# A state-space scan and a GELU feed-forward in one kernel: the first four chunks loaded, scaled and turned in two halves of 64 partitions

## The chip, the cores and the metric

The kernel runs on one core of one Trainium2 chip. The metric is device time in microseconds of one execution, as the median of several runs. A core has a matrix engine (TensorE, in the profile PE, with its weight loads PEld), a vector engine (VectorE, DVE), a scalar engine (ScalarE, ACT), a general engine (GpSimd, POOL) and a queue that issues most transfers (SyncE, SP). Each engine runs its instructions in order; between engines only semaphores order the work. Matrix results land in PSUM, which has eight banks of 128 partitions x 2 KB; VectorE and ScalarE copy them ("evict" them) to the on-chip memory SBUF.

## What is computed

Two parts follow each other. The first is a scan with 4 batches, 8 heads, 768 positions, head size 32 and state size 16. With `cum` the running sum of `log a` inside a chunk it is

```python
CB = np.einsum('bhin,bhjn->bhij', Cc, Bc)
M = CB * L                       # L = exp(cum_i - cum_j), causal
y_intra = np.einsum('bhij,bhjd->bhid', M, xc)
y_inter = np.einsum('bhin,bhnd->bhid', Cc, state) * decay_to_i[:, :, :, None]
y[:, :, sl] = y_intra + y_inter
state = decay_full[:, :, None, None] * state + np.sum(Bx, axis=2)
...
x = np.ascontiguousarray(attn_out.transpose(0, 2, 1, 3)).reshape(B * S, H * D)
h = x @ w_in                     # 3072 x 256 by 256 x 2048
out = gelu_tanh(h) @ w_out       # 3072 x 2048 by 2048 x 256
```

The second part is most of the arithmetic: two matrix products of 3072 x 256 x 2048 each.

## The kernel before

**Tiling.** The 3072 positions are 24 chunks of 128, six to a batch, and 12 units of two chunks. A unit u passes through these steps, whose names are used from here on:

- G.u: C times B for both chunks and eight heads, into the four banks `ga` and `gb` (line 603); M.u.0 and M.u.1 multiply the two pairs of banks by the causal mask on VectorE (line 613). For unit 0 alone the second pair goes another way: GE copies a bank on ScalarE (line 618) and ME masks the copy on GpSimd (line 624) or VectorE (line 627).
- D.u gives the chunk's addition to the state; S.c updates the state of chunk c, SP.c spreads it by heads (lines 684 and 691, VectorE).
- Y.u adds M times x and C times state in bank `yb` (lines 658, 667); yev.u evicts it as bf16 into `xm`.
- s1.u.i, i = 0 to 7: four matmuls of 256 columns with two of the sixteen 128-column blocks of `w_in` (line 717) into one of two banks `hp`; gelu.u.i empties it (line 721).
- s2.c.q, q = 0 to 3: four matmuls of 256 columns with a quarter of `w_out` (line 735); oev.c evicts, store.c writes to HBM. s2.c.q needs the gelus 2q and 2q+1 of its unit and quarter q of `w_out`.

So there are 384 s1 and 384 s2 matmuls. Quarter q of `w_in` (load_wi.q, casts wi.q.0 and wi.q.1) is needed by s1.u.2q; the same for `w_out` with load_wo.q, wo.q.0 and wo.q.1.

**How B, C and x come in.** Batch 0 is split: chunks 0 to 3 are loaded first (load_bc0.1 for C, load_bc0.0 for B, load_x4 for x), with four neighbouring positions on each of the 128 partitions; chunks 4 and 5 follow (load_bc1). `a` comes twice: as `aq` for the first 512 positions, one chunk on 32 partitions, and as `a_t` for all, half a sequence on 32 partitions. clipq, Rq (a scan), tpq (a transpose) and recip0 make the weights from `aq`; mulc.0, mulc.1 and mulb scale C (in two masked copies) and B; tw.1, tw.2 and tw.0 turn them by TensorE through `ident`, ew evicts; x is cast (x4), and XX.u spreads it by a 0/1 matrix `unp` to the chunks' order, XD.u stands for D.u, xn.c evicts. clip, R, tp6, recip, pe, pp, pend do the same from `a_t` for the rest. Batch 1 is turned on TensorE (mul, T, E, F, N, bn), batches 2 and 3 by transposing transfers (load_wr, load_tr, load_bn).

**What sets the order.** The text ORDERED lists every step once. Each engine gets its steps in that order. `name:E` puts a step on another engine (A ScalarE, D VectorE, P GpSimd); `~n` are n idle blocks of 128 columns of a zero weight on TensorE; `+n` are idle blocks inside an s1 step. Steps that are not named otherwise run on the engine given in `add`. Transfers of `load_*` are issued from SP, or from ScalarE with `:A`.

Up to s1.2.0, the first feed-forward matmuls of unit 2, the order before names two s2 steps (s2.0.0.0 and s2.0.1.0). All of unit 0's s2 steps go by quarters over its two chunks into one bank `o_ps`; from unit 1 on a chunk's four quarters follow each other.

Of the kernel before, what the change touches and what calls it, by code (L numbers as in the profile page):

```python
# [23 lines left out]
load_bc1.0 load_wo.0 wi.3.0:D gelu.0.1 wi.2.1 s1.0.3 load_x.2 SP.2 pe wi.3.1 gelu.0.2 load_bc.1.1  # L24
gelu.0.3 tp6.2 s1.0.4 load_bc.1.0 gelu.0.4 load_x.3 load_wo.1 xn.3 s1.0.5 s1.0.6 Y.1 gelu.0.5 pp
tp2 gelu.0.6 tp6.3 recip1 s1.0.7 S.1.1 yev.1.0.2 mul1.0:P mul1.1:P tp6.1 pend gelu.0.7 s1.1.0
wo.0.1 T1.0 s1.1.1 T1.1 gelu.1.0 bh1 N1 gelu.1.1 s1.1.2 tp6.0 s1.1.3+10 bn1 ce1.1 load_wo.2
castx.2.None SP.3 wo.0.0 ce1.0 gelu.1.2 gelu.1.3 G.2 s1.1.4 recip.1.4 s1.1.5 gelu.1.4 M.2.1
mul.1.1:P s2.0.0.0.o D.2 M.2.0 load_x.4 gelu.1.5 s2.0.1.0.o s1.1.6 T.1.1 gelu.1.6 S.2.0 s1.1.7
SP.4 Y.2 mul.1.0 yev.2.0.2:D gelu.1.7 wo.1.0 wo.1.1 T.1.0 E.1.1:A castx.3.None:A s1.2.0 wo.2.0  # L30
s1.2.1 E.1.0 wo.2.1 load_wo.3 load_bc.2.1 N.1 gelu.2.0 F.1 s1.2.2 bn.1:D G.3 gelu.2.1 gelu.2.2 D.3
s1.2.3 s2.0.0.1.o S.3.0 S.3.1 load_bc.2.0 gelu.2.3 s1.2.4 M.3.1 s2.0.1.1.o s1.2.5 SP.6 gelu.2.4
s1.2.6 M.3.0 gelu.2.5 wo.3.0:D gelu.2.6 s2.0.0.2.o castx.4.None s1.2.7 Y.3 gelu.2.7 wo.3.1:D
s2.0.1.2.o S.4.0 yev.3.0.2 S.4.1 s2.0.0.3.o oev.0 load_x.5 s1.3.0 s1.3.1 mul.2.1 s2.0.1.3.o
load_wr.2.1 load_x.6 gelu.3.0 gelu.3.1 s1.3.2 oev.1:D SP.8 s1.3.3 s2.1.0.0.o gelu.3.2 M.4.0
gelu.3.3 SP.7 s2.1.0.1.o s2.1.0.2.o s2.1.0.3.o oev.2:D s1.3.4 s1.3.5 s2.1.1.0.o gelu.3.4 M.4.1
mul.2.0:P castx.5.None:A s2.1.1.1.o Y.4 S.5.0 s2.1.1.2.o load_wr.2.0 s2.1.1.3.o load_tr.2.1
load_bn.2 oev.3:D gelu.3.5 s1.3.6 s1.3.7 s2.2.0.0.o yev.4.0.2 load_tr.2.0 gelu.3.6 s1.4.0 SP.9
M.5.1 gelu.3.7 s2.2.0.1.o store.0 store.2 gelu.4.0 s1.4.1 castx.6.None:A s1.4.2 SP.10 s2.2.0.2.o
load_x.7 s2.2.0.3.o gelu.4.1 oev.4:D gelu.4.2 s1.4.3 s1.4.4 load_bc.3.1 s2.2.1.0.o s2.2.1.1.o  # L40
s2.2.1.2.o gelu.4.3 gelu.4.4 s2.2.1.3.o s1.4.5 oev.5 s1.4.6 gelu.4.5 M.5.0 s2.3.0.0.o F.2 store.1
Y.5 s2.3.0.1.o s2.3.0.2.o yev.5.0.2 gelu.4.6 s2.3.0.3.o s1.4.7 S.6.0 gelu.4.7 load_bc.3.0 S.6.1
store.3 s1.5.0 oev.6:D SP.12 s2.3.1.0.o gelu.5.0 s1.5.1 s2.3.1.1.o gelu.5.1 castx.7.None:A
mul.3.1:P s2.3.1.2.o s1.5.2 gelu.5.2 M.6.1 s2.3.1.3.o s1.5.3 M.6.0 Y.6 oev.7:D S.7.0 gelu.5.3
load_x.8 s1.5.4 S.7.1 s2.4.0.0.o s2.4.0.1.o s1.5.5 SP.13 gelu.5.4 load_wr.3.1 yev.6.0.2
castx.8.None store.4 load_x.9 gelu.5.5 SP.14 s2.4.0.2.o s2.4.0.3.o oev.8 s1.5.6 s1.5.7 mul.3.0
castx.9.None s2.4.1.0.o gelu.5.6 load_wr.3.0 gelu.5.7 M.7.0 s2.4.1.1.o s1.6.0 M.7.1 load_tr.3.1
# [38 lines left out]
def kernel(  # L86
# [62 lines left out]
    def load_bc0(i):  # L149
        nc.sync.dma_start(out=BC0[0][:, i], in_=(B, C)[i][0, :, 0:R4 * Q, :]  # L150
                          .rearrange("h (p r) n -> p h (r n)", r=R4))
# [5 lines left out]

    def load_aq(i, eng):
        (nc.scalar if eng == "ACT" else nc.sync).dma_start(out=aq_t[32 * i:32 * i + 32], in_=a_rows(i * Q, Q))  # L159
# [22 lines left out]
    def load_x4():  # L182
        nc.sync.dma_start(out=x4_t, in_=x[0, :, 0:R4 * Q, :].rearrange("h (p r) d -> p h (r d)", r=R4))  # L183
# [35 lines left out]
    def c_wz():  # L219
        nc.vector.memset(wz, 0.0)  # L220

    def c_zero():
# [5 lines left out]
        nc.vector.memset(unp, 0.0)
# [755 lines left out]
```

## Time and profile before

| | |
|---|---|
| median of 3 runs | 118.47 us (118.43 to 118.48) |
| span of the profiled execution | 116.9 us |
| TensorE clock granted | 1.00 throughout |
| TensorE matmul / weight load busy | 110.1 us / 92.0 us |
| VectorE / ScalarE / GpSimd busy | 69.4 us / 72.1 us / 21.4 us |
| DMA | 42,800 packets and 15.64 MB on SP's queue |

The profile gives no time of the profiled execution other than its span; what lies around the span is seen only in the difference to the runs.

How to read it: the span runs from the first to the last instruction of the core. In a line of the timeline the first number is the start, the second the length, then come the engine (SPq and ACTq are the transfers that SP and ScalarE issue), the line of the kernel, the operation with its output and inputs, their shapes, how many are merged into the line, and in brackets the idle time ahead of it with what ended it. Matmuls overlap: each has a latency of some 0.2 us beyond its share of the stream, so eight that follow each other closely show a length that is longer than the time they take up. The chain of waits gives that time.

### The profile page before, as it was taken

What the parts mean: (1) busy time and instruction counts of PE and PEld (TensorE: products, weight loads), DVE (VectorE), ACT (ScalarE), POOL (GpSimd) and SP (SyncE); (2) the same over time, 40 slices, a digit from 0 to 9 for tenths busy, and PEclk for the clock granted to TensorE, in tenths of its full rate; (3) what the DMA queues carried; (4) which work ended last, traced back from release to release, by engine and by line L of the source; (5) the groups of instructions that cost most, each with busy time, mean ns of one, the idle gap of its engine ahead of it and who ended that gap; (6) DMA issues with size and microseconds to landing.
All of it is one profiled execution on the core that took longest, in us unless ns stands there. A gap on an engine that the chain in (4) does not pass through costs nothing.

```text
span 116.9 us, 3379 instructions
## 1 busy us (share of the span) xinstructions
PE 110.1 (94%) x1426; PEld 92.0 (79%) x1426; DVE 69.4 (59%) x140; ACT 72.1 (62%) x139; POOL 21.4 (18%) x38
## 2 busy tenths in 40 slices
PE   6988999998899999999999999999999999999990
PEld 2354676776789979989898999889798998999970
DVE  5898899899785936716695583049493462101020
ACT  2249899968486459565766677828465587447501
POOL 7606816908206000052200000000000000000000
PEclk9999999999999999999999999999999999999999
DMA  0999997999983929998407472044201201101113
GB/s 26 228 332 357 281 252 178 208 288 257 305 143 90 185 47 219 213 253 200 72 25 171 121 163 63 0 140 98 40 6 63 71 0 52 43 0 50 45 47 132
DMA packets 43007, 15.97 MB, mean 137 GB/s; under 512 B 36657, under 2 KB 41457, under 8 KB 42993
## 3 DMA queue, kind: packets, MB, share of 16 engines
q1 hardware_dynamic: 42800, 15.64, 56.0%
q8 instruction: 11, 0.18, 0.6%
q10 hardware_dynamic: 192, 0.13, 0.5%
q14 instruction: 4, 0.02, 0.1%
HBM read 11.04 MB, written 3.93 MB: 128 GB/s over the span
## 4 chain that ended last, share of the span: by engine, by line
PE 75%; DMA 8%; DVE 6%; SPq 6%; issue 2%; POOL 1%; ACT 0%; DVEq 0%; POOLq 0%
PE o_ps L735 33%; PE hp L717 30%; DMA bcf<-in_B_dram 8%; PE yb L735 3%; SPq L190 3%; PE ga L603 3%; PE yb L658 2%; DVE m L613 2%; PE yb L667 2%; DVE ce L523 1%; SPq L150 1%; DVE bh L327 1%; DVE bc L484 1%; SPq L159 1%; SPq L183 1%
## 5 line engine op out<-in xcount | busy, mean ns | idle before, releaser
L721 ACT ACTIVATE gT<-hp 128x512 bf16<-128x512 f32 x96 | 54.3, 596 | 25.0 <-PE hp L717 24.6
L717 PE MATMUL hp<-xm,w_in_sb 128*128 128x256 bf16 x384 | 53.3, 273 | 0.6 <-ACT gT L721 0.4
L735 PE MATMUL o_ps<-w_out_sb,gT 128*128 128x256 bf16 x352 | 47.3, 273 | 0.0
L717 PEld LDWEIGHTS <-w_in_sb 128*128 128x128 bf16 x384 | 41.4, 114 | 3.5 <-issue 1.9
L735 PEld LDWEIGHTS <-gT 128*128 128x128 bf16 x384 | 37.0, 98 | 4.9 <-issue 1.1
L327 DVE COPY o_sb<-o_ps 128x256 f32<-128x256 f32 x13 | 5.5, 425 | 23.8 <-PE o_ps L735 20.4
L613 DVE TENSOR_TENSOR m<-ga,tri 128x1024 bf16<-128x1024 f32 x12 | 14.6, 1218 | 0.1
L613 DVE TENSOR_TENSOR m<-gb,tri 128x1024 bf16<-128x1024 f32 x11 | 13.4, 1219 | 0.7 <-PE gb L603 0.7
L323 ACT ACTIVATE o_sb<-o_ps 128x256 f32<-128x256 f32 x9 | 3.5, 385 | 9.2 <-PE o_ps L735 9.2
L705 PE MATMUL yb<-wz 128*128 128x512 bf16 (+3 forms) x23 | 7.6, 481 | 1.1 <-DVE wz L220 1.1
L691 DVE SCALAR_TENSOR_TENSOR sp_new<-s_new,pend,bmask 128x256 bf16<-128x256 f32 x17 | 7.9, 476 | 0.0
L327 DVE CAST xm<-yb 128x512 bf16<-128x512 f32 x6 | 4.1, 687 | 5.8 <-PE hp L636 4.8
L684 DVE SCALAR_TENSOR_TENSOR s_new<-s_new,pend,hp 128x64 f32<-128x64 f32 x13 | 3.6, 279 | 6.4 <-PE hp L636 6.2
L705 PEld LDWEIGHTS <-wz 128*128 128x128 bf16 x26 | 3.0, 120 | 5.1 <-issue 3.2
L667 PE MATMUL yb<-m,x 128*32 128x128 bf16 x192 | 6.1, 220 | 0.0
L603 PE MATMUL ga<-ce,bh 32*128 32x256 bf16 x48 | 4.7, 273 | 1.3 <-DVE bn L327 0.9
L484 POOL TENSOR_TENSOR bc<-bc_t,pt 128x768 bf16<-128x768 f32 x2 | 3.0, 1494 | 13.8 <-DMA bc_t<-in_C_dram 13.7
L658 PE MATMUL yb<-ce,sp_new 128*32 128x128 bf16 x160 | 5.3, 221 | 0.0
L603 PE MATMUL gb<-ce,bh 32*128 32x256 bf16 x48 | 4.7, 273 | 0.0
L735 PE MATMUL yb<-w_out_sb,gT 128*128 128x256 bf16 x32 | 4.6, 273 | 0.0
L667 PEld LDWEIGHTS <-x 128*32 128x32 bf16 x192 | 3.8, 97 | 0.8 <-issue 0.8
L323 ACT ACTIVATE xm<-yb 128x512 bf16<-128x512 f32 x6 | 3.6, 595 | 1.1 <-PE hp L636 1.1
(115 smaller groups left out, 79.5 us busy)
## 6 DMA issues: line engine op xcount, KB each, us to landing
out_dram<-o_sb SPq DMA_DIRECT2D x24, 128.0 KB, 1.9
x_t<-in_x_dram SPq DMA_DIRECT2D x20, 128.0 KB, 3.9
wf<-in_moe_w_in_dram SPq DMA_DIRECT2D x4, 512.0 KB, 6.7
wf<-in_moe_w_out_dram SPq DMA_DIRECT2D x4, 512.0 KB, 5.5
bc_t<-in_C_dram SPq DMA_DIRECT2D x3, 384.0 KB, 5.8
bc_t<-in_B_dram SPq DMA_DIRECT2D x3, 384.0 KB, 5.5
scr<-bc SPq DMA_DIRECT2D x4, 192.0 KB, 2.2
x_t<-in_x_dram SPq DMA_DIRECT2D x1, 512.0 KB, 5.8
```

Of the source, the lines that this page charges most:

```text
L323: nc.scalar.activation(o, i, AF.Copy)
L327: nc.vector.tensor_copy(out=o, in_=i)
L484: (nc.gpsimd if eng == "POOL" else nc.vector).tensor_tensor(out=d["bc16"][:, i], in0=d["bc"].rearrange("p i h (r n) -> p i r h n", r=R6)[: ...
L603: nc.tensor.matmul(out=gbank(g)[:, 256 * k:256 * k + 256], lhsT=bh_of(2 * u + k)[gs], rhs=ce_of(2 * u + k)[gs], start=True, stop=True, til ...
L613: nc.vector.tensor_tensor(out=m_of(u)[:, 2 * i:2 * i + 2].rearrange("p g k e t -> p (g k e) t"), in0=gx[i].rearrange("p g (k t) -> p (g k) ...
L658: nc.tensor.matmul(out=y4[32 * j:32 * j + 32, k, w], lhsT=sp[:, 32 * h:32 * h + 32], rhs=ce_of(gc)[:, h % 2], start=first(j), stop=False, ...
L667: nc.tensor.matmul(out=y4[32 * j:32 * j + 32, k, w], lhsT=X16[u][:, k, 32 * h:32 * h + 32], rhs=m[:, h // 2, h % 2, :], start=first(j), st ...
L691: nc.vector.scalar_tensor_tensor(out=sp_new.rearrange("p (g d) -> p g d", g=4), in0=(XN[0][:, H * D:H * D + 64] if gc == 0 else state[("s" ...
L705: nc.tensor.matmul(out=t[:, 0:m * 128], lhsT=wz, rhs=w3.to_broadcast([128, m, 128]), start=True, stop=True, skip_group_check=True)
L717: nc.tensor.matmul(out=hp[:, j * T:(j + 1) * T], lhsT=w_in_k[:, w, q, k], rhs=xm[:, w, u * T:(u + 1) * T], start=(w == 0), stop=(w == 1))
L721: nc.scalar.activation(gts[u][:, 2 * i:2 * i + 2], hps.pop((u, i)).rearrange("p (j t) -> p j t", j=2), AF.Gelu_apprx_tanh)
L735: nc.tensor.matmul(out=ops[gc], lhsT=gts[u][:, fi, k * Q:(k + 1) * Q], rhs=w_out_sb[:, fi, :], start=(fi == 0 and (u > 0 or k == 0)), stop ...
```

## The change

The loads, scalings and turns of chunks 0 to 3 are split in two halves of 64 partitions (h = 0 holds chunks 0 and 1, h = 1 chunks 2 and 3): load_bc0.i.h, load_x4.h, mulc.e.h, mulb.h.k (also split by position), tw.i.h, ew.h.i, x4.h.k. So unit 0 needs the first halves only. The turn by TensorE is now a matmul of 64 rows with a part of `ident` instead of a transpose, and its result is fp32.

With it go:

- the unp and selp copies move from VectorE to ScalarE, constants for the scan (`ends`) to GpSimd;
- `a_t` lies on 128 partitions (a quarter of a sequence and the start of the next on 32), loaded by four transfers on SP; tp6 is one instruction, recip one per batch, the masks of pe and pp grow to 16 columns;
- Y.0 and yev.0 are split in two (Yw.0.w); unit 1 uses GE and ME as well; tw of the second half and XX.1 use banks of `ga` and `gb`;
- unit 1's s2 steps go by quarters too, both chunks in the bank `yb`;
- load_x.u.k loads one chunk at a time;
- ORDERED is new throughout: among other things the quarters of `w_out` are loaded ahead of x for units 2 and 3, and 15 s2 steps stand ahead of s1.2.0.

Lists on the steps named `behind` have no effect on what is run.

```diff
 ORDERED = """
-load_aq.0 load_aq.1 load_aq.2 load_aq.3 c_wz load_bc0.1 c_ident c_m4 c_sel c_tri c_zero load_bc0.0
-c_unp load_a.0:A clipq load_x4 Rq tpq recip0 c_cz mulc.0 ~59 tw.1 load_wi.0 c_warm load_a.1:A
-ew.1.1:A mulc.1 c_bmask c_m8 tw.2 mulb ~4 tw.0 peq ew.0.2:A clip ew.0.1 load_wi.1 ew.0.0:A ew.1.2
-c_par ~2 G.0 x4.1 ew.1.0 M.0.0 ~1 ppq GE.2 pendq x4.0:P XX.0 ME.2 XD.0 GE.3 xn.1 ME.3 xn.0:D
-load_wi.2 SP.0 ~17 Y.0 wi.0.1:A wi.0.0:A S.0.0 yev.0.0.2 wi.1.1 XX.1 wi.1.0:A R XD.1 S.0.1
-load_wi.3 S.1.0 s1.0.0 SP.1 xn.2 load_bc1.1 wi.2.0 gelu.0.0 G.1 s1.0.1 s1.0.2 M.1.1 M.1.0
...
+c_wz c_ident c_sel c_sub load_aq.1 load_aq.3 c_zero load_aq.0 load_aq.2 clipq c_unz Rq tpq c_m4
+c_warm c_cz c_selp load_bc0.0.0 load_bc0.1.0 load_x4.0 c_bmask load_bc0.0.1 recip0 peq mulc.0.0
+mulc.1.0 load_bc0.1.1 c_az ~44 c_unp mulb.0.0:P tw.1.0 mulb.0.1:P ew.0.1:A tw.0.0 tw.2.0 load_wi.0
+ew.0.2 ~2 ppq ew.0.0 load_x4.1 ~3 G.0 load_wi.1 x4.0.1 c_tri x4.0.0:D GE.0.2 mulb.1.0:P pendq ~4
+XX.0 GE.0.3 wi.0.0:A mulc.1.1:P load_wi.2 load_bc1.0 xn.1 M.0.0 XD.0 xn.0:D ~7 tw.2.1 SP.0
+mulb.1.1:P mulc.0.1:P ME.0.3:D tw.0.1 ~2 tw.1.1 ew.1.1:A ME.0.2 S.0.0 ew.1.0 wi.0.1:D ~5 Yw.0.0
+S.0.1 wi.1.0:D Yw.0.1 ew.1.2 yev.0.0.1 yev.0.1.2 SP.1 load_wi.3 load_a.2 load_wo.0 load_a.1 load_a.3
+x4.1.1:P G.1 wi.1.1:D M.1.0 load_a.0 c_ends x4.1.0:P s1.0.0+4 GE.1.3 GE.1.2 load_bc.1.0 s1.0.1 c_par
+wi.2.0:D XX.1 load_bc.1.1 c_m16 ME.1.3 gelu.0.0 s1.0.2 gelu.0.1 wi.2.1 s1.0.3 XD.1 xn.2:D ME.1.2:D
+S.1.0 gelu.0.2 s1.0.4 gelu.0.3 SP.2 xn.3 wi.3.1:D s1.0.5 wo.0.1:D clip R Y.1 wi.3.0 load_wo.1
+gelu.0.4 s1.0.6 gelu.0.5 load_bc1.1 yev.1.0.2 gelu.0.6 wo.0.0 s1.0.7 gelu.0.7 s2.0.0.0.o s1.1.0
+gelu.1.0 tp6 pe s1.1.1 s2.0.1.0.o tp2 S.1.1 recip.1 s1.1.2 gelu.1.1 s1.1.3 s2.1.0.0.o gelu.1.2
+recip1 s1.1.4 gelu.1.3 mul.1.1 load_wo.2 mul.1.0:P load_x.2.0 T.1.0 gelu.1.4 pp s2.1.1.0.o T.1.1
+wo.1.0 mul1.1:P s1.1.5 E.1.0:A wo.1.1:D mul1.0 s2.1.0.1.o T1.0 load_wo.3 s2.0.0.1.o bh1:D E.1.1:A
+pend gelu.1.5 T1.1 s1.1.6 wo.2.0 N1 SP.3 ce1.0 s1.1.7 ce1.1 gelu.1.6 gelu.1.7 wo.2.1 bn1:D
+load_x.2.1 wo.3.0 s2.1.1.1.o F.1 s2.1.0.2.o wo.3.1:A G.2 M.2.0 s2.1.1.2.o s2.0.1.1.o s2.1.0.3.o
+s2.1.1.3.o castx.2.None:A D.2 load_x.3.0 M.2.1 oev.2 oev.3 S.2.0 N.1 s2.0.0.2.o load_x.3.1 SP.4
+bn.1:D s2.0.1.2.o Y.2 castx.3.None:D G.3 load_x.4.0 D.3 load_x.4.1 load_bc.2.0 S.3.0 yev.2.0.2 S.3.1
+s2.0.0.3.o s1.2.0 oev.0 gelu.2.0 s1.2.1 s2.0.1.3.o gelu.2.1 s1.2.2 M.3.0 gelu.2.2 s1.2.3 gelu.2.3
...
-    def load_bc0(i):
-        nc.sync.dma_start(out=BC0[0][:, i], in_=(B, C)[i][0, :, 0:R4 * Q, :]
+    def load_bc0(i, h):
+        nc.sync.dma_start(out=BC0[0][HP * h:HP * h + HP, i], in_=(B, C)[i][0, :, 2 * Q * h:2 * Q * h + 2 * Q, :]
                           .rearrange("h (p r) n -> p h (r n)", r=R4))
...
+    def load_x4(h):
+        nc.sync.dma_start(out=x4_t[HP * h:HP * h + HP], in_=x[0, :, 2 * Q * h:2 * Q * h + 2 * Q, :]
+                          .rearrange("h (p r) d -> p h (r d)", r=R4))
...
+    def load_a(i):
+        n = min(AL, S - i * QL)
+        nc.sync.dma_start(out=a_t[32 * i:32 * i + 32, 0:n], in_=a_of(i * QL, n))
...
+    def f_tp6():
+        turn(rt, r_t[:, 0:QL], R6)
...
+    def f_mulb(h, k, eng):
+        ps, rs = half(h), slice(2 * k, 2 * k + 2)
         (nc.gpsimd if eng == "POOL" else nc.vector).tensor_tensor(
+            out=bc0s[0][ps, 0, rs], in0=BC0[0][ps, 0].rearrange("p h (r n) -> p r h n", r=R4)[:, rs],
+            in1=over(rt0[0][ps, rs, 0:H]).to_broadcast([HP, 2, H, N]), op=ALU.mult)
...
+        for r in range(R4):
+            src = cz[ps, i - 1, r] if i else bc0s[0][ps, 0, r]
+            nc.tensor.matmul(out=t[:, HP * r:HP * r + HP], lhsT=src.rearrange("p h n -> p (h n)"),
+                             rhs=ident[ps, ps], start=True, stop=True,
+                             tile_position=(HP * h, 0), skip_group_check=True)
...
+    def f_x4(h, k, eng):
+        ps, ks = half(h), slice(4 * k, 4 * k + 4)
+        copy(eng, x4b[ps, ks].rearrange("p h r d -> p h (r d)"), x4_t[ps, ks])
...
-            XN[c] = pso.tile([128, 512], FP32, name="o_ps") if c in (0, 3) else psh.tile([128, 512], FP32, name="hp")
+            XN[c] = gx[1][:, k] if u else pso.tile([128, 512], FP32, name="o_ps") if k == 0 else psh.tile([128, 512], FP32, name="hp")
...
-            if u == 0:
+            if u < 2:
                 if k == 0:
-                    ops["0"] = pso.tile([128, 512], FP32, name="o_ps")
-                ops[gc] = ops["0"][:, k * d_model:(k + 1) * d_model]
+                    ops["u"] = yb if u else pso.tile([128, 512], FP32, name="o_ps")
+                ops[gc] = ops["u"][:, k * d_model:(k + 1) * d_model]
...
-        for k, q in [(k, q) for q in range(4) for k in range(2)] if u == 0 else [(k, q) for k in range(2) for q in range(4)]:
+        for k, q in [(k, q) for q in range(4) for k in range(2)] if u < 2 else [(k, q) for k in range(2) for q in range(4)]:
```

More of the change, by code (lines that the diff above doesn't have):

```diff
@@ L24 @@
[L24 to L47, printed above, removed]
@@ L347, in f_Rq @@
     def f_Rq():
-        scan(rq_t, acq, Q)
+        scan(rq_t, acq, endq, Q)
     def turn(o, i, n):
@@ L942 @@
         y.deps = [d for d in y.deps if d is not y]
+    for s in steps.values():
+        if "A" in s.alt and s is not cwarm and s not in aq:
+            s.behind = [*s.behind, cwarm]
     pools = {"hp": 2, "o": 1, "ga": 1, "gb": 1, "yb": 1, "wf": WFB, "xl": XL, "ld": 2, "ob": 6, "st": 4, "sp": 4}
```

347 lines of the change are left out of this document (199 added, 148 removed).

## The prediction

> **What bounds the kernel now.** I read the busy time by stage first, then the count of the two large matmul groups in the same stages, then the timeline of the first 12.5 us, and last the DMA issues with their landings. The stages are the fill-in, the work to the first feed-forward matmul (12.45), a mixed stage to 30.26, the rest, and the tail.
>
> ```profile
> core 0: us, PE busy (x) PEld busy (x) DVE busy (x) ACT busy (x) POOL busy (x), PEclk, DMA share, GB/s
> 3.40:12.45 9.05, 8.20 (x144) 4.16 (x142) 8.10 (x25) 5.32 (x15) 4.19 (x10) 1.00 1.09 323
> 12.45:30.26 17.81, 15.92 (x216) 12.00 (x215) 15.99 (x30) 14.63 (x30) 9.89 (x15) 1.00 1.04 242
> 30.26:114.30 84.04, 83.61 (x1065) 74.94 (x1064) 43.43 (x76) 51.00 (x95) 4.73 (x4) 1.00 0.44 99
> 114.30:116.90 2.60, 0.00 (x0) 0.00 (x0) 0.00 (x0) 0.00 (x0) 0.00 (x0) 1.00 0.32 106
> ```
> ```profile
> 30.26:114.30 84.04, 42.40 (x308) 33.40 (x308) 1.00 0.44 99
> ```
> ```profile
> 30.26:114.30 84.04, 49.62 (x376) 36.28 (x376) 1.00 0.44 99
> ```
> ```profile
> 32.13 0.87 PE hp L717 x8
> ```
>
> The first block is all work by stage (length, then busy time and instruction count of each engine), the second the s1 matmuls of line 717 alone, the third the s2 matmuls of line 735 alone; the last line is a piece of the chain of waits. From 30.26 to 114.30 TensorE is busy 83.61 of 84.04 us: that stage has nothing to win but work done earlier. It holds 308 + 376 = 684 of the 2 x 384 large matmuls, at 0.87 / 8 = 0.109 us each, 74.6 us; the other 9.5 us are Y, G and D of nine units, 1.05 us a unit. Before 30.26 only 84 large matmuls were done in 17.8 us, 9.2 us of TensorE, while the DMA share was 1.04 and VectorE busy 15.99. So the time is decided by **how many large matmuls are done before the stream closes up**.
>
> That gives one equation. The changed order puts 15 s2 quarters and 16 s1 steps, 31 x 4 = 124 large matmuls, ahead of s1.2.0, with G.3 and D.3 done, which is the old state at 30.26 apart from 40 more matmuls (40 x 0.109 = 4.37 us). If X is when s1.2.0 starts in the new kernel, the gain is 30.26 + 4.37 - X = 34.6 - X. The tail (2.60) stays: the last s2 quarters, one eviction and one store.
>
> **The front, by halves.**
>
> ```profile
> 0.81 0.89 ACTq L159 DMA_DIRECT2D aq_t<-in_a_dram  x2
> ```
> ```profile
> aq_t<-in_a_dram ACTq DMA_DIRECT2D x2, 16.0 KB, 2.0
> ```
> ```profile
> 3.32 0.27 DVE L228 MEMSET unp<- 128x256 uint32 x1
> ...
> 3.78 0.57 DVE L270 COPY unp<-sub 128x32 bf16<-128x32 bf16 x4
> 4.25 0.21 DVE L337 TENSOR_SCALAR acq<-aq_t 128x128 f32<-128x128 f32 x1
> 4.50 0.42 DVE L340 TENSOR_TENSOR_SCAN rq_t<-acq,ends 128x128 f32<-128x128 f32 x1
> 4.96 0.41 DVE L351 STREAM_TRANSPOSE rt<-rq_t 128x128 f32<-128x128 f32 x1
> 5.40 0.35 DVE L357 RECIPROCAL pt<-rt 128x32 f32<-128x32 f32 x1
> 5.84 0.76 DVE L418 TENSOR_TENSOR cz<-bcf,pt 128x256 bf16<-128x256 f32 x2
> 6.52 0.68 DVE L425 TENSOR_TENSOR bc0s<-bcf,rt 128x512 bf16<-128x512 f32 x1
> ...
> 7.31 0.34 DVE L337 TENSOR_SCALAR ac<-a_t 64x384 f32<-64x384 f32 x1
> ...
> 8.57 1.22 DVE L613 TENSOR_TENSOR m<-ga,tri 128x1024 bf16<-128x1024 f32 x1
> ...
> 12.83 0.48 DVE L691 SCALAR_TENSOR_TENSOR sp_new<-s_new,pendq,bmask 128x256 bf16<-128x256 f32 x1
> ...
> 15.75 0.42 DVE L327 CAST w_in_sb<-wf 128x512 bf16<-128x512 f32 x1
> ```
> ```profile
> 8.65 0.63 ACT L323 ACTIVATE x4b<-x_t 128x512 bf16<-128x512 f32 x1 [0.30 <-DMA x_t<-in_x_dram]
> 9.19 0.58 ACT L618 ACTIVATE ge<-gb 128x512 bf16<-128x512 f32 x1
> 9.67 0.17 ACT L323 ACTIVATE pendq<-hp 128x4 f32<-128x4 f32 x1
> ...
> 10.41 0.38 ACT L323 ACTIVATE x<-hp 128x256 bf16<-128x256 f32 x1
> ```
> ```profile
> 8.13 0.28 PE L603 MATMUL ga<-ce,bh 32*128 32x256 bf16 x2 [0.36 <-DVE par L275]
> ...
> 12.50 0.60 PE L717 MATMUL hp<-xm,w_in_sb 128*128 128x256 bf16 x4
> ...
> 14.67 1.09 PE L717 MATMUL hp<-xm,w_in_sb 128*128 128x256 bf16 x8 [0.20 <-ACT gT L721]
> ...
> 16.96 0.29 PE L658 MATMUL yb<-ce,sp_new 128*32 128x128 bf16 x8
> ```
> ```profile
> 18.54 0.62 POOL L444 TENSOR_TENSOR bc0s<-bcf,rt 128x256 bf16<-128x256 f32 x1 [3.59 <-DVE rt L351]
> ```
>
> These are the timeline of single engines, and one line of DMA landings (median from issue to landing).
>
> The second aq load of a queue is issued near 1.27 and lands at 3.3, but VectorE takes it only at 4.25, behind the memsets and the unp copies. Those copies go to ScalarE, so clipq can start at 3.35. Ahead of the first mulc now stand clipq 0.21, the unp memset 0.27, the scan 0.42, the transpose 0.41, the reciprocal 0.35, and c_m4 and peq (small ones, no more than the memset's 0.27 each); with the gaps of the rows, 2.35: mulc starts at 5.7, hardly before the old 5.84. What helps is that mulb leaves VectorE (0.68) for GpSimd, where its two pieces (0.62 each, as row 18.54) run during recip0 and mulc. An instruction on 64 partitions costs between half and all of a full one; I take all of it, since 64x384 at 0.34 against 128x128 at 0.21 follows the columns, not the partitions. So two mulc 0.84, the 64-row matmuls of tw 0.25 and ew 0.38 put G.0 at 7.25 (was 8.13).
>
> Then ScalarE's queue decides, and it has grown: x4.0.1 0.63, GE.0.2 and GE.0.3 0.58 each, pendq 0.17, a weight cast 0.62 (as x4), xn.1, ew.1.1, ew.1.2 and two yev halves at 0.38 each, together 4.5 us. **s1.0.0 starts at about 12.0** (7.2 + 4.5, some gaps, a short wait for wi.0), 0.5 us earlier. But unit 1's GE.1.3 and GE.1.2 (1.16) now stand ahead of gelu.0.0, which starts at 13.1; now it can start when the four matmuls of row 12.50 end, at the same 13.1. The front's gain is spent there.
>
> VectorE's queue then sets Y.1. From M.0.0 at 7.6 it runs two M (1.22), two xn (0.42), three SP (0.48), two ME, ew.1.0, four weight casts (0.42), three S and c_par (0.2 to 0.3 each): 8.8 us, with gaps 9.2. ME on VectorE isn't in the trace; between 0.42 (a cast of 512 columns) and 0.61 (half an M) I take 0.5. So Y.1 can start at 16.9, just where it starts now (16.96).
>
> **From Y.1 to s1.2.0.** Y.1 takes 0.55, s1.0.6 to s2.0.0.0 three times 0.44, and s1.1.0 waits for gelu.0.6 behind yev.1: 18.95. From there the s2 quarters fill the 0.2 us that TensorE now loses per pair of gelus (row 14.67). 8 s1 and 14 s2 steps at 0.437 are 9.6; Y.2, G.3, D.3 1.05; G.2, D.2 0.45; three sets of six transposes and three of two, each half a large matmul, with pp 1.5. Sum 12.6, X = 31.5 without a wait; I allow 0.4 for Y.2 behind SP.4 and the evictions of unit 1's s2, which share bank yb with Y.2: **X = 31.9, gain 2.7**.
>
> `a` now lies on 128 partitions: one 192-column transpose in place of four and reciprocals by batch save VectorE near 2 us. But its loads move from ScalarE's queue to SP's, behind wi.3 and wo.0, so clip and scan R come near 17.5 (now R is done near 12); behind them on VectorE wait tp6, mul.1.1 and the eviction of batch 1. T.1.0 is due near 21.8, and tp6, pe, tp2, the reciprocals and mul.1.1 (0.95 or so) take 3.5 us from 18.2, as an estimate from columns by the rows above: in time by nothing. The cover is s1.1; without it this costs up to 1 us. The constants c_ends, c_m16 cost nothing on GpSimd, which row 18.54 shows idle for 3.59 us; if GpSimd is late, x4.1.0 and so XX.1 are.
>
> **The weights' turn.** Loads are the other condition.
>
> ```profile
> 1.73 0.42 SPq L150 DMA_DIRECT2D bcf<-in_C_dram  x1
> ...
> 2.81 0.75 SPq L183 DMA_DIRECT2D x_t<-in_x_dram  x1
> ...
> 24.48 2.87 SPq L194 DMA_DIRECT2D wf<-in_moe_w_out_dram  x1
> ```
> ```profile
> bcf<-in_C_dram SPq DMA_DIRECT2D x1, 256.0 KB, 3.5
> ...
> x_t<-in_x_dram SPq DMA_DIRECT2D x1, 512.0 KB, 5.8
> ...
> wf<-in_moe_w_out_dram SPq DMA_DIRECT2D x1, 512.0 KB, 6.3
> ```
> ```profile
> 26.27 1.17 POOL L325 CAST w_out_sb<-wf 128x512 bf16<-128x512 f32 x2 [2.90 <-DMA wf<-in_moe_w_out_dram]
> ...
> 27.67 1.29 POOL L325 CAST w_out_sb<-wf 128x512 bf16<-128x512 f32 x2 [0.23 <-DMA wf<-in_moe_w_out_dram]
> ```
>
> wo.1 lands at 26.27 and wo.2 at 27.67, 1.4 us apiece; wo.3 lands at 24.48 + 6.3 = 30.8, so the two x halves between them took 30.8 - 27.67 - 1.4 = 1.7 us, 0.85 each. The new order puts x.2, x.3 (four halves, 3.4 us) and bc1.1 (about 1) behind wo.1 and `a` (0.4) ahead: wo.1 lands at 22.3, wo.2 (after bc1.1) 24.7, wo.3 (after half of x.2) 26.9, the rest of x.2 27.8. With 0.6 to 1.2 us of casts they are wanted at 23.8, 26.3, 27.9 and 28.8 in the count above. All fit, the last ones by some **0.4 us**. Where x.2 is later, its cast waits on ScalarE, and behind it the evictions oev.2 and oev.3, which must empty bank yb for Y.2. SP waits nowhere in between, and batch 1's loads, now ahead of wo.1, land near 20.
>
> What the trace doesn't show is a load to 64 partitions: six of them, 1.05 MB. From 5.2 (1.73 + 3.5) to 8.6 (2.81 + 5.8) 786 KB landed, so 1.05 MB takes 4.5 us. At worst the halves run at half the rate, +4.5 us on all later loads; at best nothing, since the DMA share of 1.09 over that stage says engines are busy with packets, whose number stays; a gain is excluded as engines are never idle there. I take 0: same packets, and C's half with B's are what C was alone, landing near 5.2, before mulc wants it at 5.7.
>
> [...]
>
> **Sum.** The profiled execution spans 116.90 (the end of the last stage); 116.9 - 2.7 = 114.2. The median of the runs, 118.47, is 1.57 above that span. The profile gives no time of its own execution around the span, so I take the 1.57 for what lies around it and carry it over: **115.7 us**.
>
> **Rivals.**
> 1. VectorE and the gelus are not late, and s1.2.0 follows s1.0.0 without a gap: 12.0 + 31 x 0.437 + 1.3 (XX.1, XD.1, Y.1) + 3.0 = 29.85, a gain of 4.8: 113.7 is the floor. With half the 0.2 us gelu waits of unit 0 left, X = 30.4, **114.2 us**. For it: the new order has no idle fills after s1.0.0. Against: the full queues above.
> 2. The half loads lose part of their rate, midway 2.2 us; less the 0.4 us of slack, 1.8: **117.5 us**. For it the saturated DMA share, against it the packets.
> 3. Slower: they run at half the rate. Everything behind x4.1 is 4.5 us late, wo.1 to x.2 with it; less 0.4, X = 36.0, **119.8 us**. It decides against the change from 3.1 us of lateness on (2.7 + 0.4). [...]
> 4. The halves do not bring s1.0.0 forward (ScalarE's 4.5 us longer, wi.0 late). Since Y.1 hangs on VectorE, up to 0.4: 116.1, inside the forecast's own range.
>
> **Chances.** Forecast with rival 4, 114.8 to 116.6: 0.48. Rival 1: 0.18. Rival 2: 0.17. Rival 3: 0.12. Between 2 and 3, no difference: 0.05. A measurement of this kernel tells 0.2% from no change, 0.24 us. Faster 0.82, same 0.05, slower 0.13. From the floor 113.7 to rival 2 with 0.5 us over it, 118.0, lie 8 in 10.
>
> **What would show it.** Right: first s1 near 12.0, Y.1 near 16.9, s1.2.0 (the 65th s1 matmul) near 31.9 with some 60 s2 matmuls before it, and TensorE full from there. Wrong: x4.0 landing after 7 us or wo.1 after 23 (rivals 2, 3); Y.1 before 16 (rival 1); a TensorE gap at T.1.0 or Y.2 over 1 us; an idle stretch after s1.2.0.

## The result, and the profile after

The changed kernel takes **123.83 us** (median of 4 runs, 123.78 to 123.91) against 118.45 of the kernel before on the same chip: 1.047 times as long, 95% interval 1.0447 to 1.0499. Forecast was 115.7. The profiled execution of the changed kernel took 123.78 with a span of 121.7. An execution more than 1.5% above the fastest of its kernel counts as slow and is left out of the ratios below, but not out of the medians.

The first view of the changed kernel has the same four stages as before (length, then busy time and count of each engine, granted clock, DMA share, GB/s), cut where the first and the 65th s1 matmul start and where TensorE ends.

```profile
core 0: us, PE busy (x) PEld busy (x) DVE busy (x) ACT busy (x) POOL busy (x), PEclk, DMA share, GB/s
3.40:17.50 14.10, 9.39 (x121) 4.15 (x120) 8.61 (x23) 5.37 (x18) 8.39 (x23) 0.79 0.99 256
17.50:38.90 21.40, 20.30 (x283) 16.04 (x282) 17.65 (x38) 14.91 (x31) 9.47 (x11) 0.98 1.03 227
38.90:119.10 80.20, 79.30 (x1026) 71.27 (x1024) 40.47 (x66) 55.05 (x103) 5.47 (x6) 1.00 0.40 89
119.10:121.70 2.60, 0.00 (x0) 0.00 (x0) 0.00 (x0) 0.00 (x0) 0.00 (x0) 0.84 0.32 110
```

From the 65th s1 matmul on TensorE is full again (79.30 of 80.20 us) and the tail is 2.60, as forecast. The loss lies ahead of it: the first s1 starts at 17.56 (12.0 forecast, 12.50 before), the 65th at 38.91 (31.9 forecast), with 60 s2 matmuls done by then. Call that start X, as in the prediction.

The chain of waits of the changed kernel (start, length, what; the pieces in order of time) names the place, and the timelines of ScalarE and TensorE show it.

```profile
5.20 6.64 DMA wf<-in_moe_w_in_dram
11.84 0.02 issue
11.86 0.02 ACT w_in_sb L347
11.88 0.51 issue
12.39 0.38 ACT x L347
12.77 0.04 issue
12.81 0.20 PE hp L617
```
```profile
8.52 0.60 ACT L658 ACTIVATE ge<-gb 128x512 bf16<-128x512 f32 x1
11.86 0.63 ACT L347 ACTIVATE w_in_sb<-wf 128x512 bf16<-128x512 f32 x1 [2.73 <-DMA wf<-in_moe_w_in_dram]
12.39 0.37 ACT L347 ACTIVATE x<-hp 128x256 bf16<-128x256 f32 x1
```
```profile
12.81 0.20 PE L617 MATMUL hp<-x4b,bc0s 32*32 32x64 bf16 x1 [3.92 <-ACT x L347]
14.01 0.39 PE L470 MATMUL gb<-ident,cz 64*128 64x64 bf16 x4
...
17.56 1.50 PE L761 MATMUL hp<-xm,w_in_sb 128*128 128x256 bf16 x8
```

ScalarE finishes GE.0.3 at 9.1 and then stands for 2.73 us at the cast wi.0.0, whose weights land only at 11.8. Behind it in ScalarE's order stands xn.1, whose input has long been there. And TensorE's XD.0 stands behind xn.1: it writes the bank hp that xn.1 reads. So TensorE waits 3.92 us for a copy of 0.37 us that waits behind a cast nobody wants yet: s1.0.0 is 5 us away. What followed the wait is seen in the stages of the same kernel around it:

```profile
9.00:12.00 3.00, 0.00 (x0) 0.00 (x0) 0.23 (x1) 0.27 (x2) 2.38 (x4) 0.94 1.01 203
12.00:15.00 3.00, 2.19 (x45) 1.05 (x45) 1.69 (x5) 0.76 (x2) 1.11 (x6) 0.50 1.07 322
15.00:18.00 3.00, 3.00 (x42) 1.39 (x42) 2.79 (x7) 1.93 (x6) 2.10 (x9) 0.50 1.09 351
18.00:21.00 3.00, 2.99 (x57) 2.19 (x56) 1.44 (x4) 2.28 (x5) 2.54 (x4) 0.92 1.13 274
```

After three idle microseconds the granted clock is 0.50 from 12 to 18 us, and the work between XD.0 and s1.0.0 runs at half speed: two blocks of 512 zero columns take 0.86 us in the chain of waits from 13.22 on, 0.43 each, against 0.22 for as many columns at a clock of 1.00 (twice the 0.109 us that a matmul of 256 columns took in the kernel before). By the 0.94 the clock fell near 11.6, 2.8 us after the end of TensorE's last matmul (8.89), and by the 0.92 it was back near 18.5, 5.7 us after the start of the next (12.81); both times are estimates that take it as either 1.00 or 0.50 within those two stages.

The loads are later too. SP's timeline and the landing (last number) of the first weights in the changed kernel:

```profile
5.20 0.62 SPq L199 DMA_DIRECT2D wf<-in_moe_w_in_dram  x1
```
```profile
wf<-in_moe_w_in_dram SPq DMA_DIRECT2D x1, 512.0 KB, 6.6
```

Before, the first of these was issued at 3.61. The five half loads ahead of it now take 0.63 to 0.72 us of SP each (the rows of whole ones, of twice the bytes, show 0.42 to 0.75), so 1.6 us are lost by issuing alone.

### The profile page after: what moved, and what is told of

Its sections match the earlier page's. It is cut to its first block, busy times and chain, and to the rows that moved or that the text cites. A ratio compares the mean times of both kernels' runs of the same rounds, so it can differ in the third digit from the quotient of the medians.

```text
span 121.7 us, 3422 instructions
## 1 busy us (share of the span) xinstructions
PE 111.3 (91%) x1432; PEld 92.4 (76%) x1432; DVE 67.7 (56%) x132; ACT 77.0 (63%) x153; POOL 25.9 (21%) x49
## 2 busy tenths in 40 slices
DMA packets 43151, 16.00 MB, mean 131 GB/s; under 512 B 36736, under 2 KB 41600, under 8 KB 43136
## 4 chain that ended last, share of the span: by engine, by line
PE 76%; DVE 8%; DMA 5%; SPq 3%; issue 3%; ACT 1%; DVEq 0%
PE hp L761 32%; PE o_ps L779 27%; DMA wf<-in_moe_w_in_dram 5%; PE yb L779 4%; PE ga L639 3%; PE yb L708 2%; SPq L154 2%; PE yb L699 2%; PE yb L749 2%; DVE pe L419 1%; DVE rt L374 1%; DVE m L649 1%; DVE bc L520 1%; ACT ch L347 1%; SPq L166 1%
## 5 line engine op out<-in xcount | busy, mean ns | idle before, releaser
L761 PE MATMUL hp<-xm,w_in_sb 128*128 128x256 bf16 x384 | 54.1, 275 | 0.0
L779 PE MATMUL o_ps<-w_out_sb,gT 128*128 128x256 bf16 x320 | 44.6, 273 | 0.0
L649 DVE TENSOR_TENSOR m<-gb,tri 128x1024 bf16<-128x1024 f32 x10 | 12.2, 1215 | 0.0
L735 DVE SCALAR_TENSOR_TENSOR sp_new<-s_new,pend,bmask 128x256 bf16<-128x256 f32 x17 | 9.9, 598 | 0.1
L779 PE MATMUL yb<-w_out_sb,gT 128*128 128x256 bf16 x64 | 9.0, 273 | 0.0
L347 ACT ACTIVATE o_sb<-o_ps 128x256 f32<-128x256 f32 x14 | 5.3, 381 | 5.7 <-PE o_ps L779 5.7
L347 ACT ACTIVATE xm<-yb 128x512 bf16<-128x512 f32 (+1 forms) x11 | 6.0, 559 | 2.9 <-PE yb L708 2.4
L351 DVE COPY o_sb<-o_ps 128x256 f32<-128x256 f32 x6 | 2.5, 425 | 7.7 <-PE o_ps L779 7.2
L349 POOL CAST x<-x_t 128x512 bf16<-128x512 f32 x4 | 2.5, 631 | 19.9 <-PE gb L639 10.2
L520 POOL TENSOR_TENSOR bc<-bc_t,rt 128x768 bf16<-128x768 f32 x3 | 4.5, 1496 | 8.0 <-DVE pe L418 4.0
```

What stands on the lines that cost most here:

```text
L347: nc.scalar.activation(o, i, AF.Copy)
L520: (nc.gpsimd if eng == "POOL" else nc.vector).tensor_tensor(out=d["bc16"][:, i], in0=d["bc"].rearrange("p i h (r n) -> p i r h n", r=R6)[: ...
L649: nc.vector.tensor_tensor(out=m_of(u)[:, 2 * i:2 * i + 2].rearrange("p g k e t -> p (g k e) t"), in0=gx[i].rearrange("p g (k t) -> p (g k) ...
L735: (nc.gpsimd if eng == "POOL" else nc.vector).scalar_tensor_tensor(out=sp_new.rearrange("p (g d) -> p g d", g=4), in0=(XN[0][:, H * D:H * ...
L761: nc.tensor.matmul(out=hp[:, j * T:(j + 1) * T], lhsT=w_in_k[:, w, q, k], rhs=xm[:, w, u * T:(u + 1) * T], start=(w == 0), stop=(w == 1))
L779: nc.tensor.matmul(out=ops[gc], lhsT=gts[u][:, fi, k * Q:(k + 1) * Q], rhs=w_out_sb[:, fi, :], start=(fi == 0 and (u > 1 or k == 0)), stop ...
```

## The experiments

Two theories for the 7.0 us by which X missed its forecast. **The order:** the cast wi.0.0 ahead of xn.1, and TensorE at a granted clock of 0.50 after it. **The loads:** halves to 64 partitions land later, and everything follows. A third came up on the way: VectorE's work on `a`. X and the span are of one profiled execution of each kernel, and these are compared below; the medians of e3, e6 and e11 come from runs 1.7 to 3.0 us apart.

| kernel | loads | cast wi.0.0 | idle blocks added | first s1 | 33rd s1 | X | span | median us | ratio to before, 95% |
|---|---|---|---|---|---|---|---|---|---|
| changed | half | before xn.1 | none | 17.56 | 24.53 | 38.91 | 121.7 | 123.83 | 1.0447–1.0499 |
| e1 | half | behind yev.0.1 | none | 15.52 | 23.80 | 37.74 | 120.5 | 121.79 | 1.0259–1.0346 |
| e2 | full | before xn.1 | none | 15.82 | 22.92 | 36.87 | 119.5 | 121.40 | 1.0212–1.0315 |
| e3 | half | before xn.1 | 66 before XD.0 | 15.39 | 22.32 | 36.50 | 119.3 | 122.37 | 1.0230–1.0387 |
| e5 | half | before xn.1 | 15 at the start, 66 before XD.0 | 15.73 | 22.53 | 36.63 | 119.4 | 121.62 | 1.0236–1.0334 |
| e6 | full | before xn.1 | 15 at the start | 15.46 | 22.35 | 36.31 | 119.0 | 121.96 | 1.0193–1.0370 |
| e7 | full | behind yev.0.1 | 15 at the start | 13.59 | 20.19 | 35.21 | 117.9 | 119.77 | 1.0069–1.0141 |
| e11 | half | behind yev.0.1 | 15 at the start | 13.66 | 21.59 | 37.03 | 119.8 | 122.70 | 1.0303–1.0428 |
| e9 | as e7 | as e7, pe ahead of tp6 | as e7 | 13.85 | 20.44 | 34.16 | 116.8 | 118.80 | 0.9981–1.0046 |
| e10 | as e9 | right behind xn.1 | as e9 | 12.89 | 19.63 | 32.91 | 115.6 | 117.72 | 0.9904–0.9963 |
| e12 | half | as e11, pe ahead, c_ends early | as e11 | 13.34 | 21.55 | 35.29 | 118.1 | 120.28 | 1.0130–1.0248 |

All of them do the same 60 s2 matmuls ahead of X. Idle blocks are matmuls on zeros that keep TensorE busy. The kernel before, in the same batches, had medians of 118.28 to 118.45.

**e1_cast_later**

```diff
-XX.0 GE.0.3 wi.0.0:A mulc.1.1:P
+XX.0 GE.0.3 mulc.1.1:P
-yev.0.0.1 yev.0.1.2 SP.1
+yev.0.0.1 yev.0.1.2 wi.0.0:A SP.1
```

> The changed kernel with one step moved: the ScalarE cast wi.0.0, which waits for the first weight load, goes from ahead of xn.1 to behind yev.0. Queue theory (the cast holds xn.1, and XD.0 on TensorE waits for xn.1): XD.0 starts near 9.2 us instead of 12.8, s1.0.0 near 13 (the landing of wi.0 near 11.9 plus a cast of 0.62) instead of 17.6, the granted clock stays 1.00, and the time is 119 to 120 us. Load theory (the half loads make everything late and the place of the cast is no matter): s1.0.0 moves by less than 1 us, 123 us or more.

X falls from 38.91 to 37.74 only, the first s1 by 2.04. XD.0 runs from 9.4 on in place of 12.8, as expected. But the granted clock, expected to stay at 1.00, is 0.52 from 9 to 12 us and 0.50 from there to 18, and TensorE now waits 0.40 us for mulc.1.1, which GpSimd does late. The stages of e1 around the fall:

```profile
6.00:9.00 3.00, 2.65 (x34) 1.48 (x35) 2.36 (x5) 2.29 (x7) 1.19 (x3) 1.00 0.90 211
9.00:12.00 3.00, 1.92 (x41) 0.85 (x40) 1.72 (x5) 0.37 (x2) 1.59 (x3) 0.52 0.91 205
```

TensorE was busy for 2.65 of the 3 us before, and its listed gaps from 3.6 to 9.5 us are 0.33 and 0.57 us. So here the clock fell without the long wait; what made it fall is open. Nor does this execution stand for all of e1: the other three have spans of 119.7 to 119.8 against its 120.5, at clocks of 0.97 to 1.00 against 0.96. The order is part of the loss, not all of it.

**e2_full_loads**: B, C and x by one load of 128 partitions each, three in place of six.

```diff
-out=BC0[0][HP * h:HP * h + HP, i], in_=(B, C)[i][0, :, 2 * Q * h:2 * Q * h + 2 * Q, :]
+out=BC0[0][:, i], in_=(B, C)[i][0, :, 0:R4 * Q, :]
```

> The changed kernel with B, C and x of the four chunks each loaded by one transfer to 128 partitions, in the place of the first halves; the work by halves stays. Load theory: wi.0 is issued near 3.7 us instead of 5.2 and lands near 10 instead of 11.9, the wait on ScalarE shrinks from 2.7 to about 0.9 us, TensorE's gap from 3.7 to about 1.8 us, which may leave the clock at 1.00; s1.0.0 near 13.5, 119 to 120 us. If 64-partition loads cost nothing: wi.0 still lands near 11.9 and the time stays within 0.5 us of 123.8.

X is 2.04 us earlier than in the changed kernel. Each theory taken alone leaves the kernel slower than before.

**e3_fill** and **e5_fill_both**: the cast stays in its bad place, but TensorE gets idle blocks to do while XD.0 waits; e5 has 59 blocks in place of 44 at the start as well.

```diff
-xn.1 M.0.0 XD.0 xn.0:D
+xn.1 M.0.0 ~66 XD.0 xn.0:D
-c_az ~44 c_unp
+c_az ~59 c_unp
```

> The changed kernel with 66 idle blocks (3.5 us) on TensorE ahead of XD.0, which cover the gap of 9.05 to 12.8 us; loads and casts are as they were. Clock theory (the idle gap halves the clock from 12 to 18.5 us, and work on the path runs at half speed there): the clock stays 1.00, XD.0 still starts near 12.8, s1.0.0 near 15.2 instead of 17.6, 121 to 121.8 us. If the half clock only covers waits for VectorE and ScalarE: the time stays within 0.5 us of 123.8.

> The changed kernel with idle blocks alone: 59 instead of 44 at the start, as in the kernel before, and 66 ahead of XD.0. Clock theory: with 44 blocks the first busy stretch ends at 5.4 us, close to where TensorE turns from 427 to 213 ns per 512 columns, so some executions stay slow; with 59 all runs agree within 0.5 us, near 121.2 us. If the run-to-run spread of the version with 66 blocks alone (121.4 to 124.4) has another cause, the spread stays 2 to 3 us.

XD.0 starts as late as before (12.84 in e5 against 12.81); what changes is the speed behind it (mean granted clock of the execution 1.00 against 0.969). X falls by 2.28 (e5): that is the price of the slow TensorE in the changed kernel. The runs of e3 lie between 121.4 and 124.4, those of e5 between 121.5 and 122.0. That the blocks at the start steady them is not shown: e6 and e11 have them too, and their runs lie 2.3 and 1.7 us apart. What differs between such runs is open.

**e6_full_59** and **e7_full_cast_59**: full loads with 59 blocks at the start; e7 with e1's edit as well.

> Full 128-partition loads and 59 idle blocks at the start; the cast wi.0.0 stays ahead of xn.1. Clock theory: in the version with full loads and 44 blocks TensorE ran at half speed until 17 us (256 columns took 0.40 us there), so with 59 blocks G.0 comes near 7.5 instead of 8.4, s1.0.0 near 13.5 instead of 15.8, time 119 to 119.5 us. If the half speed was not on the path: 121 us or more.

> Full loads, 59 idle blocks, and the cast wi.0.0 behind yev.0: all three causes taken away, the halves of the work kept. If they are the whole cause: s1.0.0 near 12.2, the 65th s1 matmul near 33, span 115.7, time 117 to 117.5 us, faster than before. If something else of the change is slow as well (the scan of a, 4 us of VectorE behind wo.0): 118 us or more.

With full loads and 15 more idle blocks at the start the cast's place is worth 1.87 us at the first s1 and 1.10 at X (e6 to e7). Slower matmuls have their part in this too. In e6 TensorE waits 2.08 us for xn.1, and matmuls of 256 columns take 0.39 to 0.42 us from 14.5 to 15.1, against 0.27 to 0.28 from 8.0 to 9.3; the mean granted clock of the execution is 0.984, that of e7 0.998. The wait of e6:

```profile
11.51 0.18 PE L618 MATMUL hp<-x4b,bc0s 32*32 32x64 bf16 x1 [2.08 <-ACT x L348]
```

e7's first s1 at 13.59 then waits 0.63 us for the cast in its new place, behind yev. At 119.77 us e7 stays above the kernel before, so something else is slow as well.

**e4_before_part** and **e8_before_head**: the kernel before with its three loads split in two, by 64 partitions (e4) or by 4 of 8 heads on all 128 partitions (e8): the same bytes and number of loads.

```diff
-nc.sync.dma_start(out=BC0[0][:, i], in_=(B, C)[i][0, :, 0:R4 * Q, :]
+nc.sync.dma_start(out=BC0[0][64 * h:64 * h + 64, i], in_=(B, C)[i][0, :, 256 * h:256 * h + 256, :]
```
```diff
+nc.sync.dma_start(out=BC0[0][:, i, 4 * h:4 * h + 4], in_=(B, C)[i][0, 4 * h:4 * h + 4, 0:R4 * Q, :]
```

> The kernel before with its loads of B, C and x of the four chunks each split in two of 64 partitions, one behind the other, and nothing else. Load theory: each issue takes about 0.65 us of SP, the first weight load is issued near 5.4 us instead of 3.6 and lands near 12 instead of 9.9, x lands near 9.5 to 10 instead of 8.6; time 119.5 to 121 us. If half loads cost nothing: 118.5 us.

> The kernel before with its loads of B, C and x of the four chunks each split in two by heads, on all 128 partitions: as many transfers and as many bytes in each as with the split by partitions. Port theory (64 partitions are what makes a load slow): issues of 0.3 to 0.45 us, x lands near 9, 118.5 to 119 us. Number theory (twice as many transfers is what costs): issues of 0.65 us, x lands near 10, the 121.7 us of the split by partitions.

e4 takes 121.74 us (1.0186 to 1.0328 of before) with a span of 120.2, e8 121.30 (1.0178 to 1.0303) with 119.1. So splitting the loads spoils the old kernel too, with nothing else changed. e8's time is that of the number theory (121.7), not the 118.5 to 119 of the theory that 64 partitions make a load slow; the two intervals overlap, so the times alone show no price of the 64 partitions beside that of the number. In both, matmuls of 256 columns took 0.39 to 0.42 us for a while (before: 0.27), at mean granted clocks of 0.986 (e8) and 0.972 (e4) against 1.00, so the clock has its part in these times. One row of the stage view from 3 to 12 us, for the kernel before, e8 and e4 in this order (the last two numbers are DMA share and GB/s):

```profile
3.00:12.00 9.00, 8.15 (x113) 4.12 (x111) 8.01 (x30) 5.27 (x14) 4.07 (x11) 1.00 1.06 311
```
```profile
3.00:12.00 9.00, 6.89 (x79) 3.29 (x78) 7.45 (x30) 4.56 (x12) 3.64 (x10) 0.92 0.96 261
```
```profile
3.00:12.00 9.00, 6.98 (x79) 3.21 (x78) 6.96 (x28) 4.12 (x11) 3.41 (x10) 0.99 0.84 207
```

In this stage the split by heads takes the rate from 311 to 261 GB/s, the split by 64 partitions to 207. Per busy share, the bytes move at 293, 272 and 246 GB/s: the engines stand idle more, and each byte takes longer. A load of half the partitions also held SP longer than one of half the heads: a pair took 1.31 to 1.40 us in e4 against 0.97 to 1.06 in e8.

**e11_half_cast_59**: e7 with the half loads again.

> e7_full_cast_59 with the loads of B, C and x by halves again: the half loads' own price, with the cast out of ScalarE's way and TensorE kept warm from the start. If half loads cost only their issue (wi.0 1.6 us later on SP, landing 11.8) : mulc.1.1 late by 1 to 2 us, first s1 near 14.9 to 15.5 against 13.6, 65th 36.5 to 37, time 121.0 to 121.7 against 119.8. If their price in the changed kernel is hidden elsewhere: first s1 within 0.4 of 13.6 and time within 0.4 of 119.8. If cold matmuls carried it in e1: matmuls of 512 columns at 0.21 throughout and time near 120.

The first s1 is as early as with full loads (13.66 against 13.59): at that point their lateness is hidden. It shows later. TensorE and GpSimd of e11:

```profile
15.88 0.37 PE L607 MATMUL gb<-x4b,unp 32*128 32x256 bf16 x3 [1.15 <-POOL x4b L349]
```
```profile
13.08 0.61 POOL L349 CAST x4b<-x_t 64x512 bf16<-64x512 f32 x1 [1.10 <-DMA x_t<-in_x_dram]
13.75 0.10 POOL L242 MEMSET ac<- 128x1 f32 x1
...
14.19 0.73 POOL L247 MEMSET ends<- 32x1 f32 x4
14.99 0.84 POOL L349 CAST x4b<-x_t 64x512 bf16<-64x512 f32 x1
```

The second half of x lands at 13.0. GpSimd waits for it, and c_ends (1.2 us of memsets) stands between the two casts, so XX.1 starts 1.15 us after TensorE is free for it. At X the half loads cost 1.82 us (e7 to e11) and by the medians 2.9.

**e9_pe_first**: e7 with one swap on VectorE.

```diff
-gelu.1.0 tp6 pe s1.1.1
+gelu.1.0 pe tp6 s1.1.1
```

> e7_full_cast_59 with pe one place earlier on VectorE, ahead of tp6, so that pe has run when tp6 releases GpSimd's mul.1.0. In every run of the changed kernel so far pe 128x48 took 1.50 us, beside a GpSimd mul.1.0 of 1.50 us that began 0.06 us earlier. Theory 'held beside GpSimd, on the path': pe takes 0.2 to 0.3, tp2, the reciprocals and mul.1.1 come 1.3 earlier, the 0.79 us wait ahead of T.1.1 and the 0.65 ahead of D.3 close, from the 33rd to the 65th s1 matmul 13.6 to 13.9 us in place of 15.0, 65th near 33.9, time 118.4 to 118.7 in place of 119.8. Rival 'the hold moves on': tp6 or tp2 takes the 1.3 us instead, nothing changes: 15.0, 119.8. Rival 'it is not on the path' (TensorE's own work or the loads set it): pe short, 65th within 0.3 of 35.2, 119.5 to 119.8.

What led to it: in the changed kernel and all its variants above, pe's second instruction took 1.50 us, beside a GpSimd instruction of 1.50. In the changed kernel, VectorE and GpSimd:

```profile
24.94 1.50 DVE L419 TENSOR_TENSOR pe<-pe,m 128x48 f32<-128x48 f32 x1
```
```profile
24.88 1.50 POOL L520 TENSOR_TENSOR bc<-bc_t,rt 128x768 bf16<-128x768 f32 x1 [4.05 <-DVE pe L418]
```

and in e9:

```profile
20.44 0.21 DVE L420 TENSOR_TENSOR pe<-pe,m 128x48 f32<-128x48 f32 x1
20.57 1.55 DVE L375 STREAM_TRANSPOSE rt<-r_t 128x192 f32<-128x192 f32 x5
```
```profile
21.18 1.49 POOL L521 TENSOR_TENSOR bc<-bc_t,rt 128x768 bf16<-128x768 f32 x1 [3.71 <-DVE rt L375]
```

Ahead of mul.1.0, pe takes 0.21; the transposes that now run beside it are not held (1.55 us for the five, against 0.53 and 0.99 in the changed kernel). X falls by 1.05 and the median to 118.8, level with the kernel before.

**e10_cast_mid**: e9 with wi.0.0 in the idle stretch of ScalarE between xn.1 and ew.1.1.

```diff
-yev.0.0.1 yev.0.1.2 wi.0.0:A SP.1
+yev.0.0.1 yev.0.1.2 SP.1
-xn.1 M.0.0 XD.0 xn.0:D
+xn.1 M.0.0 XD.0 wi.0.0:A xn.0:D
```

> e9 with the cast of weight quarter wi.0.0 on ScalarE between xn.1 and ew.1.1, where that engine stood idle for 1.66 us in e7, in place of behind yev. Theory 'the place of that one cast in ScalarE's order sets the first s1': wi.0 lands near 9.9, the cast is done by 10.6, first s1 about 13.0 in place of 13.6, 0.6 us earlier throughout; time 117.8 to 118.1, below the kernel before (118.4). Rival 'the loads set it': the cast waits until past 11, ew.1.1 and so Yw.0.1 come late, first s1 at 13.6 or later, time no better than e9.

```profile
9.42 0.40 ACT L348 ACTIVATE x<-hp 128x256 bf16<-128x256 f32 x1
11.10 0.63 ACT L348 ACTIVATE w_in_sb<-wf 128x512 bf16<-128x512 f32 x1 [1.28 <-DMA wf<-in_moe_w_in_dram]
11.64 0.37 ACT L348 ACTIVATE ce<-ga 128x256 bf16<-128x256 f32 x1
12.32 0.66 ACT L348 ACTIVATE xm<-yb 128x256 bf16<-128x256 f32 x2
```

The cast still waits 1.28 us for its weights in this execution (ScalarE's timeline), until 11.10, which is the sign that the rival named and not the 9.9 expected for the landing. But now xn.1 is through and nothing that is due stands behind it. First s1 at 12.89, **117.72 us** (12 runs), 0.9934 of the kernel before (0.9904 to 0.9963): the changed order, with full loads, 15 more idle blocks at the start and two instructions moved, is the fastest kernel here.

**e12_half_ends**: e11 with pe ahead of tp6 and c_ends moved to an idle stretch of GpSimd near 4 us.

```diff
-c_az ~59 c_unp
+c_az c_ends ~59 c_unp
-M.1.0 load_a.0 c_ends x4.1.0:P
+M.1.0 load_a.0 x4.1.0:P
```

> e11_half_cast_59 (half loads) with c_ends moved on GpSimd from between x4.1.1 and x4.1.0, where its 1.2 us stood behind a wait for the second half of x (until 13.08), to an idle stretch near 4 us, and with pe ahead of tp6. Theory 'half loads cost their lateness once, at x4.1, and c_ends behind it doubles that': x4.1.0 starts near 13.7 in place of 14.99, XX.1 by 14.8 in place of 15.88, 33rd s1 near 20.5 in place of 21.6, and with pe short (worth 1.05 from e7 to e9) 65th near 34.9 in place of 37.03, time 119.1 to 119.8. Rival 'the loads hold more than x4.1 up' (wi.1, `a`, wo): 65th at 36 or later, time 120.5 or more. Either way half loads stay behind the same kernel with full loads (e9, 118.8).

X 35.29 and 120.28 us, between the two expectations. x4.1.0 came earlier, but the 33rd s1 did not (21.55): the s1 steps then waited for casts of wi.1 and wi.2 (0.19 and 0.40 us), and the last of `a` landed at 20.8, where e12's chain of waits passes through it. So the half loads hold up more than x4.1, and against the full loads of e9 they still cost 1.1 us at X.

## Why the prediction was wrong

**The equation held.** It says span = X + 82.3 (114.2 - 31.9). With the measured X it gives 121.2 for the changed kernel (121.7 measured) and 115.2 for e10 (115.6); in all eleven kernels of the table it is 0.3 to 0.5 short. So the miss is X, 38.91 for 31.9: 5.56 us ahead of the first s1, nothing from there to the 33rd (6.97 for 6.95), 1.43 from the 33rd to the 65th.

**The step that failed first: "ScalarE's queue … together 4.5 us … a short wait for wi.0".** Up to there the working held: G.0 starts at 7.50 (7.25 forecast), and GE.0.3 ends at 9.1. But the step added durations of a queue and did not ask what each instruction in it waits for. The wait was 2.73 us, and its worst effect was not its length on ScalarE but who stood behind: xn.1, and through the bank hp XD.0 on TensorE. Moving that one cast brought the first s1 forward by 2.04 us (e1) and 1.87 (e6 to e7), and its better place a further 0.96 (e9 to e10). Rival 4 named "wi.0 late" but priced it at 0.4.

**"I take 0" for the half loads failed too.** The six loads were argued by packets, whose number hardly changed (43,151 in all in the changed kernel, 43,007 before). They cost 2.04 us at X in e2, 1.82 between e7 and e11, 1.13 where the order behind them was mended (e9 to e12, with c_ends moved as well). The bounds (0 to 4.5) held them; the value was wrong. Rival 2's midway 2.2 us came near in size, but that the 64 partitions are the cause is not shown: e8, on all 128 partitions, cost as much as e4 within the noise, with SP's issuing and the clock in both. Of the signs that the prediction named, wo.1 after 23 did show (18.35 + 6.3 = 24.7), and x4.0 landing after 7 us was on the edge (3.16 + 3.8 = 7.0); the loads that held up the front were wi.0 and x4.1 (5.87 + 7.8 = 13.7), which it did not list.

**A term that was missing: TensorE's clock.** The sum costs every matmul at its length at a granted clock of 1.00 (0.109 us for 256 columns). In the changed kernel an idle stretch of 3.9 us cost itself and 2.28 us more (by e5).

**"tp6, pe, tp2, the reciprocals and mul.1.1 … take 3.5 us … in time by nothing" was mis-sized.** In the changed kernel they take 4.87 (24.27 to 29.14); pe was costed by its columns and took 1.50 beside GpSimd, and the chain of waits of the changed kernel passes through it (24.94). That chain on VectorE set the stretch from the 33rd to the 65th s1: with pe ahead it fell by 1.30, from 15.02 (e7) to 13.72 us (e9), and to 13.28 in e10, against 12.95 forecast. "Without it this costs up to 1 us", said of the cover by s1.1, came near the 1.30.

**The carried 1.57** came from a median less the span of another execution. Runs with their own span stand 1.9 to 2.1 above it (123.78 and 121.7 here; a run of before 118.22 and 116.3): 0.5 us of the miss.

The steps down from the changed kernel, each with the one edit: 38.91, cast later 37.74, 15 more idle blocks at the start 37.03, full loads 35.21, pe ahead 34.16, cast in the idle stretch 32.91. They are not independent (full loads alone were worth 2.04, idle blocks against the fall of the clock alone 2.28), and the 0.71 of the blocks at the start is not shown: it starts from one execution of e1, while the other three have the span of e11's (119.7 to 119.8 against 119.8), and the same 15 blocks gained nothing from e3 to e5 (36.50 to 36.63). The last 1.0 us to 31.9 is not settled either: 0.9 of it is the first s1 at 12.89. Of the rivals none named the outcome; rival 3 had the sign and, in late loads, part of the cause, at 119.8, but its reason (half the rate) is not what the runs showed: e4's stage had 207 GB/s against 311.

## What to carry to other kernels

For each instruction moved within an engine's queue, ask when its own input lands and who stands behind it, also through a shared bank: a wait in the wrong place costs what is queued behind it, and an idle TensorE cost again in clock here (2.28 us at X). A load that is cut in two was not free here (1.1 to 2.0 us at X), though its bytes stay: count its issue time on SP and the lateness of all loads behind it. Test a slower kernel by single edits before giving up on it: here the half loads and two instructions in the wrong place hid that the rest, with 15 more idle blocks, was worth 0.7%.
